# Attention backward for one query row: from one head per tile to two heads per tile

## The chip, the cores and the metric

The kernel runs on one core of a Trainium2 chip. The metric is the device time of one launch in microseconds (us); lower is better. The time before is the median of 3 runs, 1304.23 us (1302.53 to 1307.31). The profile is one further execution, taken by the hardware profiler.

## The reference

For each of 64 heads (B = 2, H = 32) there is one query row `q`, 8192 key rows `k` and value rows `v` of 128 numbers, and one row `grad_out`, all bf16. The forward part and its gradient are computed:

```python
def _fwd_reference(q, k, v):
    scale = q.shape[-1] ** -0.5
    scores = jnp.einsum("bhqd,bhkd->bhqk", q, k) * scale
    p = _softmax(scores, axis=-1)
    return jnp.einsum("bhqk,bhkd->bhqd", p, v)

def reference(q, k, v, grad_out):
    ...
    _out, _vjp = jax.vjp(_f, q, k, v)
    _grads = _vjp(grad_out)
    _out0 = jnp.asarray(_out)
    return (_out0, *[jnp.asarray(_g) for _g in _grads])
```

Written out for one head: p = softmax(scale * K q); out = p V; dp = V grad_out; dS = p * (dp - sum(p * dp)); grad q = scale * dS K; grad K = scale * dS x q (an outer product of 8192 by 128); grad V = p x grad_out (another). K and V, 2 MB each for a head, are read once, and grad K and grad V, 2 MB each, are written once: 537 MB in all.

## The kernel before

**Layout.** A head's 8192 rows lie on 128 partitions, 64 consecutive rows to a partition, so that a partition's share is 16 KB without a break, in memory and in the tile. `kt` and `vt` hold K and V of one head; the pool has five of each (`UNITS = 5`), 160 KB of a partition. The gradients are written over them: grad K over `kt`, grad V over `vt`, and each tile is stored from where it was loaded to. All four large transfers of a head move 2 MB in 128 rows of 16 KB.

**Queues.** SP issues the loads (line 103), `kt` then `vt`; ACT issues the stores (line 278). A load waits until the store of the head that had the buffer five heads earlier has landed.

**The order of the work** is written out by hand: one turn for each head `h` (64, and a last one to finish), of eight steps `j` with two halves `u`. In a turn, head `h` (called `y`) is transposed and its scores are formed, while the head before (`x`) gets its weighted sums, outer products and stores.

- `transposes` (lines 105 to 121): 8 matmuls by the identity write 8 blocks of 128x128 to the PSUM tile `tp` (two buffers), and one copy brings them to SBUF as `ev`: on ACT, or on DVE for two of the 16 halves of a head. Steps 0 to 3 are K, 4 to 7 are V.
- `products` (123 to 138), a step later: each transposed block is the stationary operand, and a column of q or grad_out the moving one; the results are columns of `sm` (scores) and `dp`.
- `row_max`, `all_max`, `exps` (157 to 181): after the K half, the maximum over the head, and exp of the scores into `E`, with its sum.
- `deltas`, `sums`, `weights` (190 to 231), in steps 0 and 1 of the next turn: the sum of E * dp, both sums over the partitions, and from them the weights of both weighted sums and the doubled columns `P2` and `dS2`.
- `weighted_rows` (233 to 247): 32 matmuls of 512 columns for a head, in steps 0 to 3 of the next turn, into `acc`, which gathers four heads before `acc_to_sbuf` and `combine` read it.
- `outer` (265 to 275): 8 multiplications on DVE for a head, 128x2048 each, in steps 1 to 6 of the next turn: four for grad V, then four for grad K. `store` is issued at j = 4 (grad V) and j = 7 (grad K).
- `spread_rows` (140 to 155): every four heads, the q and grad_out rows are copied to all partitions.
- At j = 7 the load of head h + 3 is written into SP's queue.

So both gradients of a head are made and stored in the turn after its own.

Of the kernel before, what the change touches and what calls it, by code (L numbers as in the profile page):

```python
# [9 lines left out]
ALU = mybir.AluOpType  # L10
# [6 lines left out]
QG = 4  # L17
OG = 4
UNITS = 5
# [3 lines left out]
def kernel(  # L23
# [10 lines left out]
):  # L34
    nc = tc.nc
# [5 lines left out]
    NT = Sk // P  # L41
    assert NT * P == Sk and NT == 4 * CH and BH <= P and BH % QG == 0
    assert BH % OG == 0 and OG * 8 == 32
    NS = 2 * NT // CH
    scale = float(D) ** -0.5

# [5 lines left out]
    ones_f = const.tile([P, P], F32)  # L52
    nc.vector.memset(ones_f[:], 1.0)

    pick = const.tile([P, 4, 2, OG], F32)
    idv = ident_f[:].rearrange("p (g w k j) -> p g j w k", g=4, w=2, k=OG)
    nc.vector.tensor_copy(out=pick[:], in_=idv[:, 0])
    for g in range(1, 4):
# [8 lines left out]
    evp = ctx.enter_context(tc.tile_pool(name="ev", bufs=5))  # L67
    work = ctx.enter_context(tc.tile_pool(name="work", bufs=2))
# [4 lines left out]

    k_v = k.rearrange("b h (p n) d -> (b h) p n d", n=NT)
    v_v = v.rearrange("b h (p n) d -> (b h) p n d", n=NT)
    dk_v = out_2.rearrange("b h (p n) d -> (b h) p n d", n=NT)
    dv_v = out_3.rearrange("b h (p n) d -> (b h) p n d", n=NT)

    acc = ps_one.tile([P, 4 * D], F32, name="acc", tag="acc")
    qT_all = const.tile([P, BH], BF16)  # L80
    doT_all = const.tile([P, BH], BF16)


    rl_all = const.tile([P, 2, BH], F32)

    wz = [
        [const.tile([P, NT // 4, 32], BF16, name=f"wz{w}{k}") for k in range(OG)]
        for w in range(2)
    ]
    colsT = const.tile([P, 2, BH], BF16)  # L90
    class Head:
        pass

    heads = [Head() for _ in range(BH)]

    def load(h):
        x = heads[h]
        x.kv = [
            kvp.tile([P, NT, D], BF16, name="kt", tag="kt"),
            kvp.tile([P, NT, D], BF16, name="vt", tag="vt"),  # L100
        ]
        for dst, src in zip(x.kv, (k_v, v_v)):
            nc.sync.dma_start(out=dst[:], in_=src[h])

    def transposes(h, j, u):

        x = heads[h]
        w, c = divmod(j, NS // 2)
        tp = ps_tp.tile([P, HC, P], F32, name="tp", tag="tp")
        for i in range(HC):  # L110
            n = c * CH + u * HC + i
            nc.tensor.matmul(  # L112
                tp[:, i, :], lhsT=x.kv[w][:, n, :], rhs=ident_bf[:], start=True, stop=True
            )
        ev = evp.tile([P, HC, P], BF16, name="ev", tag="ev")
        if u and j in (0, 7):
            nc.vector.tensor_copy(out=ev[:], in_=tp[:])  # L117
        else:
            nc.scalar.copy(out=ev[:], in_=tp[:])  # L119
        x.ev = getattr(x, "ev", {})  # L120
        x.ev[j, u] = ev

    def products(h, j, u):
        x = heads[h]
        w, c = divmod(j, NS // 2)
        if c == 0 and u == 0:
            if w:
                x.dp = ps_one.tile([P, NT + 2], F32, name="dp", tag="dp")
            else:
                x.sm = ps_one.tile([P, NT + P + 1], F32, name="sm", tag="sm")  # L130
        ev = x.ev.pop((j, u))
        col = (qT_all, doT_all)[w][:, h : h + 1]
        for i in range(HC):
            n = c * CH + u * HC + i
            nc.tensor.matmul(  # L135
                (x.dp if w else x.sm)[:, n : n + 1], lhsT=ev[:, i, :], rhs=col,
# [3 lines left out]
    def spread_rows(g):  # L140

        pb = ps_tp.tile([P, QG, 2, D], F32, name="pb", tag="tp")
        for i in range(QG):
            h = g * QG + i
            nc.tensor.matmul(
                pb[:, i].rearrange("p a d -> p (a d)"),
                lhsT=ident_bf[0:BH, h : h + 1].to_broadcast([BH, P]),
                rhs=nat[:].rearrange("p a d -> p (a d)"),
                start=True,
                stop=True,  # L150
            )
        qd = rowp.tile([P, QG, 2, D], BF16, name="qd", tag="qd")
        nc.scalar.copy(out=qd[:], in_=pb[:])  # L153
        for i in range(QG):
            heads[g * QG + i].qd = qd[:, i]

    def row_max(x):
        x.mp = work.tile([P, 1], F32, name="mp", tag="mp")
        nc.vector.reduce_max(out=x.mp[:], in_=x.sm[:, 0:NT], axis=AX.X)  # L159

    def all_max(x):
        mT = x.sm[0:1, NT : NT + P]
        nc.tensor.transpose(mT, x.mp[:], ident_f[:])  # L163
        x.gm = work.tile([1, 1], F32, name="gm", tag="gm")
        nc.vector.reduce_max(out=x.gm[:], in_=mT, axis=AX.X)

    def exps(x):
        mb = x.sm[:, NT + P : NT + P + 1]
        nc.tensor.matmul(mb, lhsT=ones_f[0:1, :], rhs=x.gm[:], start=True, stop=True)  # L169
# [4 lines left out]
        nc.scalar.activation(  # L174
            out=x.E[:],
            in_=x.sm[:, 0:NT],
            func=ACT.Exp,
            bias=negm[:],
            scale=scale,
            accum_out=x.ld[:, 0:1],  # L180
        )

    def to_weights(h, w, src):
        k = h % OG
        nc.vector.tensor_copy(  # L185
            out=wz[w][k][:, :, 16 * w + 4 * k : 16 * w + 4 * k + 4],
            in_=src[:].rearrange("p (m j) -> p m j", j=4),
        )

    def deltas(x):  # L190
        junk = work.tile([P, NT], BF16, name="junk", tag="junk")
        nc.vector.tensor_tensor_reduce(  # L192
            out=junk[:],
            in0=x.E[:],
            in1=x.dp[:, 0:NT],
            scale=1.0,
            scalar=0.0,
            op0=ALU.mult,
            op1=ALU.add,
            accum_out=x.ld[:, 1:2],  # L200
        )

    def sums(x):
        x.lsum = x.dp[:, NT : NT + 2]
        nc.tensor.matmul(x.lsum, lhsT=ones_f[:], rhs=x.ld[:], start=True, stop=True)  # L205

    def weights(h):
        x = heads[h]
        rl, rls = rl_all[:, 0, h : h + 1], rl_all[:, 1, h : h + 1]
        nc.vector.reciprocal(out=rl, in_=x.lsum[:, 0:1])  # L210
        negdelta = work.tile([P, 1], F32, name="negdelta", tag="negdelta")
        nc.vector.tensor_scalar(
            out=negdelta[:], in0=x.lsum[:, 1:2], scalar1=rl, scalar2=-1.0,
            op0=ALU.mult, op1=ALU.mult,
        )
        nc.vector.tensor_scalar(out=rls, in0=rl, scalar1=scale, scalar2=None, op0=ALU.mult)
        dSu = work.tile([P, NT], F32, name="dSu", tag="dSu")
        nc.vector.scalar_tensor_tensor(
            out=dSu[:], in0=x.dp[:, 0:NT], scalar=negdelta[:], in1=x.E[:],
            op0=ALU.add, op1=ALU.mult,  # L220
        )
        to_weights(h, 1, dSu)

        x.w2 = []
        for name, src, s in (("P2", x.E, rl), ("dS2", dSu, rls)):
            t = work.tile([P, NT, 2], BF16, name=name, tag=name)
            nc.vector.tensor_scalar(
                out=t[:], in0=src[:].unsqueeze(2).to_broadcast([P, NT, 2]),
                scalar1=s, scalar2=None, op0=ALU.mult,
            )  # L230
            x.w2.append(t)

    def weighted_rows(h, w, chunks):


        rows, k = heads[h].kv[1 - w], h % OG
        for c in chunks:
            for g in range(4):
                n = c * CH + 4 * g
                nc.tensor.matmul(  # L240
                    acc[32 * g : 32 * g + 32, :],
                    lhsT=wz[w][k][:, n // 4, :],
                    rhs=rows[:, n : n + 4, :].rearrange("p n d -> p (n d)"),
                    start=(w == 0 and k == 0 and c == 0),
                    stop=(w == 1 and k == OG - 1 and c == NT // CH - 1),
                    tile_position=(0, 32 * g),
                )

    def acc_to_sbuf(x):
        x.accsb = work.tile([P, 4 * D], F32, name="accsb", tag="accsb", bufs=1)  # L250
        nc.vector.tensor_copy(out=x.accsb[:], in_=acc[:])

    def combine(h):

        x = heads[h]
        c = ps_one.tile([P, 2, OG], F32, name="c", tag="c")
# [5 lines left out]
        own = slice(h - OG + 1, h + 1)  # L262
        nc.vector.tensor_mul(out=colsT[:, :, own], in0=c[:], in1=rl_all[:, :, own])

    def outer(h, w, i):

        x = heads[h]
        n = i * CH
# [6 lines left out]
        )  # L275

    def store(h, w, a=0, b=NT):
        nc.scalar.dma_start(out=(dv_v, dk_v)[w][h][:, a:b, :], in_=heads[h].kv[1 - w][:, a:b, :])

    def outer_and_store(h, w, i):  # L280

        outer(h, w, i)
        if h == BH - 1 and i % 2:
            store(h, w, (i - 1) * CH, (i + 1) * CH)
# [5 lines left out]
    for w in range(2):  # L290
        for t in wz[w]:
            nc.gpsimd.memset(t[:], 0.0)
# [4 lines left out]

    with tc.manual_schedule():
        for h in range(min(UNITS, BH)):
            load(h)  # L300
        for h in range(BH + 1):
            p = h - 1
            x = heads[p] if h else None
            y = heads[h] if h < BH else None
            full = h and p % OG == OG - 1
            for j in range(NS):
                for u in range(2):
                    if y:
                        transposes(h, j, u)
                    if u == 0:  # L310
                        if x and j == 1:
                            sums(x)
                        if y and j == 5:
# [67 lines left out]
```

## Time and profile before

| | |
|---|---|
| median of 3 runs | 1304.23 us |
| the profiled execution's own time | 1302.89 us |
| its span, first to last instruction | 1301.1 us |
| read from HBM, written to HBM | 268.47 MB, 268.47 MB |
| mean rate over the span | 415 GB/s |
| mean granted TensorE clock | 0.885 of full |
| copies `ev<-tp` on ACT | 896, 1025 ns each |
| copies `ev<-tp` on DVE | 128, 1224 ns each |
| outer products on DVE | 512, 1212 and 1216 ns each |
| weighted sums on PE | 2048, 415 and 476 ns each |
| issue to landing, median: `kt`, `vt`, store grad V, store grad K | 18.9, 28.5, 38.2, 40.3 us |

The page of a profile gives the busy time of each engine, the span cut in 40 slices with the DMA's share and rate, the DMA queues, the chain of work that ended last, the costliest groups of instructions with what each waited for, and the DMA issues with the time to landing. PE is TensorE's matrix multiplication, PEld its loading of the stationary operand, DVE VectorE, ACT ScalarE, SP the engine that only issues transfers. Large transfers are carried by 16 DMA engines, and each of them carries 8 of the 128 rows.

### The profile page before, as it was taken

How to read it: one execution, taken by the hardware profiler on the slowest of the kernel's cores; microseconds unless marked ns; L12 is line 12 of the kernel's file. 1: busy time of each engine (PE TensorE's matmuls, PEld its weight loads, DVE VectorE, ACT ScalarE, POOL GpSimd, SP SyncE). 2: the span in 40 equal slices, each digit the busy share in tenths (PEclk: the TensorE clock that was granted, in tenths of full speed). 3: DMA queues.
4: the chain of work that ended last, by engine and by line, in shares of the span. 5: the costliest groups of instructions: out<-in, count | busy, mean ns of one | idle time of the engine just before them, and what ended most of it. 6: DMA issues, size and time to landing. Idle time of an engine off the chain costs nothing.

```text
span 1301.1 us, 42243 instructions
## 1 busy us (share of the span) xinstructions
PE 1108.2 (85%) x18948; PEld 911.0 (70%) x18948; DVE 887.4 (68%) x1511; ACT 906.3 (70%) x1043; POOL 4.8 (0%) x16
## 2 busy tenths in 40 slices
PE   5999998988889879898898888988889888888784
PEld 5777777766767667677776767767767677677673
DVE  2887777766766767667676676766667667676566
ACT  5887778867767767676776766766668576676562
POOL 1000000000000000000000000000000000000000
PEclk9999989889887998888898888888899888898786
DMA  9999999999999999999999999999999999999986
GB/s 396 418 427 427 426 428 426 428 427 429 427 428 426 426 419 421 421 427 421 418 421 421 426 421 418 421 408 421 416 418 417 411 425 419 413 412 421 391 356 268
DMA packets 37653, 539.65 MB, mean 415 GB/s; under 512 B 4448, under 2 KB 4448, under 8 KB 4448
## 3 DMA queue, kind: packets, MB, share of 16 engines
q1 hardware_dynamic: 18432, 268.44, 49.6%
q10 hardware_dynamic: 19040, 268.51, 48.7%
q8 instruction: 148, 2.42, 0.7%
q14 instruction: 33, 0.27, 0.1%
HBM read 268.47 MB, written 268.47 MB: 413 GB/s over the span
## 4 chain that ended last, share of the span: by engine, by line
DMA 76%; PE 10%; ACT 6%; issue 4%; DVE 3%; ACTq 0%; DVEq 0%; SPq 0%
DMA out_dram<-kt 74%; PE tp L112 6%; ACT ev L119 5%; DVE ev L117 2%; PE acc L240 2%; DMA kt<-in_k_dram 1%; PE sm L135 1%; DMA nat<-in_grad_out_dram 1%; PE dp L205 0%; DVE kt L270 0%; DVE vt L270 0%; PE dp L135 0%; ACT E_f L174 0%; PE c L258 0%; PE sm L163 0%
## 5 line engine op out<-in xcount | busy, mean ns | idle before, releaser
L119 ACT CAST ev<-tp 128x1024 bf16<-128x1024 f32 x896 | 879.8, 1025 | 326.7 <-PE tp L112 270.7
L112 PE MATMUL tp<-ident_bf,kt 128*128 128x128 bf16 x4096 | 375.8, 245 | 83.3 <-DMA kt<-in_k_dram 54.8
L112 PEld LDWEIGHTS <-kt 128*128 128x128 bf16 x4096 | 281.1, 110 | 218.0 <-issue 156.4
L112 PE MATMUL tp<-ident_bf,vt 128*128 128x128 bf16 x4096 | 316.7, 221 | 60.4 <-ACT ev L119 44.3
L135 PEld LDWEIGHTS <-ev 128*128 128x128 bf16 x8192 | 332.4, 100 | 2.1 <-issue 0.2
L112 PEld LDWEIGHTS <-vt 128*128 128x128 bf16 x4096 | 260.9, 98 | 94.6 <-issue 74.2
L117 DVE CAST ev<-tp 128x1024 bf16<-128x1024 f32 x128 | 156.7, 1224 | 246.0 <-PE tp L112 237.3
L270 DVE TENSOR_TENSOR kt<-qd,dS 128x2048 bf16<-128x2048 bf16 x256 | 310.0, 1212 | 0.0
L270 DVE TENSOR_TENSOR vt<-qd,P 128x2048 bf16<-128x2048 bf16 x256 | 295.8, 1216 | 0.0
L135 PE MATMUL dp<-doT_all,ev 128*128 128x1 bf16 x4096 | 178.9, 165 | 0.1
L135 PE MATMUL sm<-qT_all,ev 128*128 128x1 bf16 x4096 | 178.6, 164 | 0.0
L240 PE MATMUL acc<-vt,wz 128*32 128x512 bf16 x1024 | 124.3, 476 | 9.3 <-DVE wz L185 9.2
L240 PE MATMUL acc<-kt,wz 128*32 128x512 bf16 x1024 | 108.2, 415 | 0.4 <-DVE wz L185 0.4
L240 PEld LDWEIGHTS <-wz 128*32 128x32 bf16 x2048 | 53.6, 95 | 21.7 <-DVE wz L185 12.4
L159 DVE TENSOR_REDUCE mp<-sm 128x1 f32<-128x64 f32 x64 | 14.4, 225 | 74.3 <-PE sm L135 74.3
L153 ACT CAST qd<-pb 128x1024 bf16<-128x1024 f32 x16 | 16.2, 1012 | 43.4 <-DMA out_dram<-kt 39.6
L210 DVE RECIPROCAL rl_all<-dp 128x1 f32<-128x1 f32 x64 | 10.8, 168 | 39.6 <-PE dp L205 39.6
L205 PE MATMUL dp<-ld,ones_f 128*128 128x2 f32 x128 | 28.4, 291 | 8.8 <-DVE ld L192 8.6
L205 PEld LDWEIGHTS dp<-ld,ones_f 128*128 128x128 f32 x128 | 24.8, 242 | 14.1 <-DVE ld L192 13.5
L171 DVE TENSOR_SCALAR negm<-sm 128x1 f32<-128x1 f32 x64 | 9.9, 154 | 23.9 <-PE sm L169 23.9
L169 PE MATMUL sm<-gm,ones_f 1*128 1x1 f32 x128 | 24.4, 257 | 0.0
L169 PEld LDWEIGHTS sm<-gm,ones_f 1*128 1x128 f32 x128 | 18.9, 184 | 6.7 <-issue 0.2
(40 smaller groups left out, 277.4 us busy)
## 6 DMA issues: line engine op xcount, KB each, us to landing
kt<-in_k_dram SPq DMA_DIRECT2D x64, 2048.0 KB, 18.9
vt<-in_v_dram SPq DMA_DIRECT2D x64, 2048.0 KB, 28.5
out_dram<-vt ACTq DMA_DIRECT2D x63, 2048.0 KB, 38.2
out_dram<-kt ACTq DMA_DIRECT2D x63, 2048.0 KB, 40.3
out_dram<-vt ACTq DMA_DIRECT2D x2, 1024.0 KB, 8.4
out_dram<-kt ACTq DMA_DIRECT2D x2, 1024.0 KB, 8.5
out_dram<-rows ACTq DMA_DIRECT2D x2, 16.0 KB, 7.4
nat<-in_q_dram ACTq DMA_DIRECT2D x1, 16.0 KB, 8.2
```

The source lines that it names most:

```text
L112: nc.tensor.matmul(tp[:, i, :], lhsT=x.kv[w][:, n, :], rhs=ident_bf[:], start=True, stop=True)
L117: nc.vector.tensor_copy(out=ev[:], in_=tp[:])
L119: nc.scalar.copy(out=ev[:], in_=tp[:])
L135: nc.tensor.matmul((x.dp if w else x.sm)[:, n : n + 1], lhsT=ev[:, i, :], rhs=col, start=True, stop=True,)
L153: nc.scalar.copy(out=qd[:], in_=pb[:])
L159: nc.vector.reduce_max(out=x.mp[:], in_=x.sm[:, 0:NT], axis=AX.X)
L169: nc.tensor.matmul(mb, lhsT=ones_f[0:1, :], rhs=x.gm[:], start=True, stop=True)
L171: nc.vector.tensor_scalar(out=negm[:], in0=mb, scalar1=-scale, scalar2=None, op0=ALU.mult)
L205: nc.tensor.matmul(x.lsum, lhsT=ones_f[:], rhs=x.ld[:], start=True, stop=True)
L210: nc.vector.reciprocal(out=rl, in_=x.lsum[:, 0:1])
L240: nc.tensor.matmul(acc[32 * g : 32 * g + 32, :], lhsT=wz[w][k][:, n // 4, :], rhs=rows[:, n : n + 4, :].rearrange("p n d -> p (n d)"), sta ...
L270: nc.vector.tensor_tensor(out=x.kv[1 - w][:, n : n + CH, :].rearrange("p n (d t) -> p n d t", t=2), in0=row.unsqueeze(1).to_broadcast([P, ...
```

## The change

Two heads, a pair, share a tile. Head 2i lies on partitions 0 to 63 and head 2i + 1 on 64 to 127, 128 consecutive rows of a head to a partition, so that a partition's share is 32 KB without a break. Every large transfer moves 4 MB in 128 rows of 32 KB. There are three tiles `kt` and three `vt` (`UNITS = 3`), 192 KB of a partition, and to make room `ev` has three buffers instead of five, and `work` one instead of two; `accsb` now takes a buffer of `ev`. The loads of the first pair are cut in four (K) and two (V).

A turn is one pair, with 16 steps: 0 to 7 transpose K, 8 to 15 V. `products` multiplies by the two columns of the pair at once; half of each result belongs to the other head and isn't read. What follows works on the rows of each head by itself (`own`, `halves`), so that many small instructions become two on 64 partitions, for a pair. Sums over the partitions use `same`, which is 1 where both partitions belong to one head.

The softmax sum is now formed by itself (`sum_exps`, step 11), so that P is known and `weighted_rows` for P runs in steps 12 to 15 of the pair's own turn. The outer products of grad V begin there too, and end in step 1 of the next turn. grad V is stored at step 3 of the next turn, grad K at step 8, and the load of pair i + 2 is written into SP's queue at step 9. `acc` is read after every pair. The stores of the last pair's pieces go out on SP's queue.

```diff
-UNITS = 5
+UNITS = 3
+EV = 3
...
-    k_v = k.rearrange("b h (p n) d -> (b h) p n d", n=NT)
...
+    def pairs_of(t):
+        rows = t.rearrange("b h s d -> (b h s) d")
+        return rows.rearrange("(i p n) d -> i p n d", p=P, n=NT)
+
+    k_v, v_v, dk_v, dv_v = (pairs_of(t) for t in (k, v, out_2, out_3))
...
+        for dst, src, parts in zip(x.kv, (k_v, v_v), (1, 1) if i else (4, 2)):
+            n = NT // parts
+            for a in range(0, NT, n):
+                nc.sync.dma_start(out=dst[:, a : a + n, :], in_=src[i][:, a : a + n, :])
...
-        if u and j in (0, 7):
+        if u and s in (8, 9, 10, 12):
             nc.vector.tensor_copy(out=ev[:], in_=tp[:])
...
-                (x.dp if w else x.sm)[:, n : n + 1], lhsT=ev[:, i, :], rhs=col,
+                (x.dp if w else x.sm)[:, 2 * n : 2 * n + 2], lhsT=ev[:, i, :], rhs=cols,
...
+    def own(t, k):
+
+        return t[halves[k], 0 : 2 * NT].rearrange("p (n k) -> p k n", k=2)[:, k]
...
+    def sum_exps(x):
+        x.lsum = x.sm[:, 2 * NT + P + 1 : 2 * NT + P + 2]
+        nc.tensor.matmul(x.lsum, lhsT=same[:], rhs=x.ld[:, 0:1], start=True, stop=True)
...
+    def to_weights(w, src, s):
+        for k, hf in enumerate(halves):
+            a = 8 * w + 4 * k
+            nc.vector.tensor_scalar(
+                out=wz[w][hf, :, a : a + 4], in0=src[hf, :].rearrange("p (m j) -> p m j", j=4),
+                scalar1=s[hf, :], scalar2=None, op0=ALU.mult,
+            )
...
+    def weights_v(x):
+        x.rl = work.tile([P, 1], F32, name="rl", tag="rl", bufs=2)
+        nc.vector.reciprocal(out=x.rl[:], in_=x.lsum)
+        to_weights(0, x.E, x.rl)
+        x.w2 = [twice("P2", x.E, x.rl[:])]
...
+    def weighted_rows(x, w, c):
+
+
+        for g in range(4):
+            m = 4 * c + g
+            nc.tensor.matmul(
+                acc[32 * g : 32 * g + 16, :],
+                lhsT=wz[w][:, m, :],
+                rhs=x.kv[1 - w][:, 4 * m : 4 * m + 4, :].rearrange("p n d -> p (n d)"),
...
     def acc_to_sbuf(x):
-        x.accsb = work.tile([P, 4 * D], F32, name="accsb", tag="accsb", bufs=1)
+        x.accsb = evp.tile([P, 4 * D], F32, name="accsb", tag="ev")
...
+    OUT_V = {13: (0,), 14: (1, 2), 15: (3, 4), 16: (5, 6), 17: (7,)}
+    OUT_K = {19: (0, 1), 20: (2, 3), 21: (4,), 22: (5, 6), 23: (7,)}
...
+        for i in range(NP + 1):
+            x = pairs[i - 1] if i else None
+            y = pairs[i] if i < NP else None
+            for s in range(NS):
                 for u in range(2):
                     if y:
-                        transposes(h, j, u)
+                        transposes(y, s, u)
                     if u == 0:
-                        if x and j == 1:
-                            sums(x)
...
+                        if x and s == 1:
+                            sum_deltas(x)
...
+                        if y and s == 11:
+                            sum_exps(y)
+                    if y and s:
+                        products(y, s - 1, u)
+                    elif x and s == 0:
+                        products(x, NS - 1, u)
+                    if x and 2 <= s < 6:
+                        weighted_rows(x, 1, 2 * (s - 2) + u)
+                    if y and s >= 12:
+                        weighted_rows(y, 0, 2 * (s - 12) + u)
+                if x and s == 0:
                     deltas(x)
+                if x and s == 1:
+                    weights_k(x)
+                if y and s == 8:
                     row_max(y)
+                if y and s == 11:
+                    weights_v(y)
+                    spread_rows(y)
+                for t, o in ((x, s + NS), (y, s)):
+                    if t:
+                        for w, at in enumerate((OUT_V, OUT_K)):
+                            for c in at.get(o, ()):
+                                outer(t, w, c)
+                if x and s == 6:
+                    acc_to_sbuf(x)
+                if x and s == 7:
+                    combine(x)
+                if x and x.i < NP - 1 and s in (3, 8):
+                    store(x, s // 8, nc.scalar)
+                if x and s == 9 and UNITS <= i + 2 < NP:
+                    load(i + 2)
```

## The prediction

> **What bounds the kernel now.** I read the page first, for the busy shares and the chain of work that ended last:
>
> ```profile
> PE 1108.2 (85%) x18948; PEld 911.0 (70%) x18948; DVE 887.4 (68%) x1511; ACT 906.3 (70%) x1043; POOL 4.8 (0%) x16
> ...
> q8 instruction: 148, 2.42, 0.7%
> ...
> DMA 76%; PE 10%; ACT 6%; issue 4%; DVE 3%; ACTq 0%; DVEq 0%; SPq 0%
> ```
>
> No engine is full, and three quarters of the chain are transfers. The chain in order of time has two regimes:
>
> ```profile
> 56.64 1.01 ACT ev L119
> ...
> 73.94 1.02 ACT ev L119
> ...
> 1011.59 40.25 DMA out_dram<-kt
> ...
> 1051.90 37.05 DMA out_dram<-kt
> 1088.96 3.42 issue
> 1092.37 40.41 DMA out_dram<-kt
> ```
>
> Up to 205 us it is computation, 17.30 us a head (56.64 to 73.94). From then on it steps from store to store, two heads each: 80.78 us for four heads (1011.59 to 1092.37), and 890.3 us for the 44 heads from 283.0 to 1173.3, so **20.23 us a head**. Computation has 2.9 us a head to spare there. What holds the DMA to 20.23 us? The windows:
>
> ```profile
> 100.00:200.00 100.00, 91.59 (x1667) 74.98 (x1666) 77.44 (x134) 78.84 (x90) 0.00 (x0) 0.97 1.01 427
> 1100.00:1200.00 100.00, 86.54 (x1507) 71.42 (x1504) 68.67 (x118) 71.45 (x83) 0.00 (x0) 0.90 1.00 416
> ...
> 1262.00:1264.00 2.00, 1.76 (x32) 1.26 (x28) 1.27 (x2) 0.42 (x2) 0.00 (x0) 1.00 1.11 475
> 1264.00:1266.00 2.00, 1.85 (x34) 1.41 (x34) 1.45 (x10) 1.16 (x2) 0.00 (x0) 1.00 0.56 229
> 1266.00:1268.00 2.00, 2.00 (x44) 1.63 (x40) 2.00 (x2) 1.90 (x3) 0.00 (x0) 1.00 0.08 33
> 1268.00:1270.00 2.00, 2.00 (x44) 1.56 (x40) 2.00 (x3) 1.90 (x3) 0.00 (x0) 1.00 0.06 25
> 1270.00:1272.00 2.00, 1.80 (x38) 1.51 (x37) 1.76 (x4) 1.95 (x3) 0.00 (x0) 1.00 0.10 33
> ```
>
> The last two columns are DMA share and GB/s. At 427 GB/s a head's 8.39 MB would take 19.6 us, and the rate falls later. From 1266 to 1272, 25 to 33 GB/s at a share of 0.06 to 0.10 is the work of one engine of 16 (427/16 = 27): fifteen have finished and wait for one. The packet records say the same all along: of a load's 16 end markers near 1005 us fifteen come by 1006.8 and the last at 1011.5, and these last ones follow at 1011.5, 1021.6, 1031.6 and 1041.6. So **one engine is late, and it sets the pace**. A 16 KB packet starts 607 ns after the one before on its engine, so 32 of them need 19.42 us a head; the late one needs some 0.8 us more. The likeliest extra is the instruction fetch (148 packets of 16 KB, 2.3 a head, each lasting 0.88 to 1.0 us); the change leaves the count of instructions as it is.
>
> The span of before is then: 2.3 us until data flow, 64 x 20.23 = 1294.7, and 4.1 at the end. The run took 1.8 us more than its span, and the median is 1.3 above that run.
>
> **The change, part by part.**
>
> *Rows of 32 KB.* The records give 306 ns from start to start for 8 KB packets and 607 for 16 KB, so one packet less saves 2 x 306 - 607 = 5 ns. A pair saves 32 of them on each engine, 0.16 us, and four end markers of 14 ns, 0.06 us: 40.46 - 0.22 = **40.24 us a pair**, 1287.7 for 32 (7 us gained). Bounds: no gain if the rows still go as 16 KB packets (7 us worse), and the 427 GB/s of the early windows if larger transfers free the kernel from its late engine (16.86 MB with fetches, 39.5 us a pair, 24 better).
>
> The Trainium skill, "SBUF — State Buffer", section "The DMA setup-cost knee", says that every transfer pays some 2 us whatever its size, so that larger ones gain. By that rule 128 transfers less would give 256 us; here transfers queue behind each other, at a share of 1.00, and the sum doesn't use it.
>
> *Compute in a pair's turn.* It must fit into 40.24 us. Rows of the compute-bound stretch: halves with `weighted_rows` start their transposes 1.06 us apart (35.45, 36.52, 37.58); the eight halves of V take 8.0 us; the wait for `sums` adds 0.8 a head. So two heads need 34.6. `products` stays 256 matmuls, bound by their weight loads (100 ns each, 165 with the matmul), so a second column costs nothing; `weighted_rows` stays 64 of 512 columns. Changed for a pair: one wait for sums less (-0.8). `combine` 8 matmuls, 1.04 us, for each pair and not for four heads (+0.5). In step 2 PE waits for `wz` of dS: DVE runs deltas (0.6), outers 5 and 6 (2.4) and weights_k up to `wz` (1.4) after the last products, 4.4 us; PE comes there after 3.3 (three halves and the sum): +1.1, with ACT's copies queued behind it. `accsb` holds an `ev` buffer through step 7, so copies wait for products (0.35 each) and step 8 for `combine`: +0.7, bounds 0 and 1.5. `spread_rows` now passes `tp` for each pair: +0.3. Two Exp with 0.24 us of accumulator reading are as many as before; strided reading of twice the columns adds 0.07 us to each of some ten: +0.7. Sum **37.1 us**, bounds 35.5 and 40: hidden by the DMA with 3.1 to spare, where before had 5.8. Without that cover each us costs 31. DVE's 16 outers and four copies stay (24.3 us a pair), the small operations go from 5.8 to about 5.6 us.
>
> The clock: after waits the granted clock is 0.50 (687 to 690 us, following a wait of 2.6 us), mean 0.86 to 0.90 in those stretches. A longer turn collects its slack in longer waits; until the slack is eaten that costs nothing. "TensorE: Matmul & The Clock Gate", Part 1, puts the fall to half rate after an idle window of about 3.4 us and says the same is needed to rise again. Every such window would cost 1.7 us, 41 us over 24 pairs if it were on the path; the slack takes it.
>
> *Filling.* Before, ten loads of 2 MB keep the DMA busy until stores come, and V follows K soon. Now a load of pair i + 2 waits for the store of grad K of pair i - 1. Compute starts at about 8.5 us, not 12 (the nat transfers pass 8 KB packets, not 16), turn 0 takes 35.7 (32 halves, no weighted sums in half of them), and grad V is issued 10.4 us into a turn, grad K 21.5. Loads of three pairs and both stores of pair 0, 33.6 MB, end at 81; the next store, V of pair 1, is issued at 44.2 + 37.1 + 10.4 = 91.7. So nothing is queued at 81, and from landing to data takes some 3.3 us (a load issued at 910.6 shows its first packets at 913.3). Likewise at 124.5 against 128.8, and at 168 against 165.9, nearly. **+7 us**, bounds 3 (a turn of 35.5) and 12. From pair 5 on a store is queued in time.
>
> *Moved loads and stores.* V and K stores on ACT's queue stand behind outer products that end by step 3 and 8 as DVE's times above add up; so no copies wait behind them. ACT's present waits there (39.6 + 16.7 us for landing stores) go, but were in turns that wait for `kt` anyway: 0.
>
> *End.* From the last load's issue (x) the late engine has 33.6 MB, 80.5 us. `kt` lands at x + 22; the last turn takes 38; then products 1.0, deltas 0.5, two outers 2.35, weights 1.8, nine outers 10.5 and accsb 0.7, and the last 1 MB store (now on SP's queue, where nothing else is left) needs 2.5 to its first packet, 2.5 for the data and 1.5 to land: x + 83.5. That is 3.0 beyond the late engine's own work, and the two small rows behind it add 1.5, as part of the 4.1 of before: **4.5 us**, bounds 0 and 12.
>
> **Sum:** 2.3 + 7 + 1287.7 + 4.5 = 1301.5 for the span, with 3.1 for launch and median 1304.6. Gains and costs cancel; as compute has less cover than before, I put the forecast at **1306**, with 1291 to 1319 as its own range (rows -0/+7, filling -4/+5, end -4.5/+7.5).
>
> **The rivals.**
>
> *Faster: the late engine no longer sets the pace.* For: 427 GB/s up to 400 us, and deeper queues. Against: its markers follow at 10.1 us early (201.6, 211.8, 222.0) and late. 32 x 39.5 + 2.3 + 7 + 4.5 + 3.1 = **1281**.
>
> *Slower: PE's turn sets the pace.* Place: steps 2 and 7 to 8, where PE waits in order for DVE and for `ev`. It decides from 39.8 us a turn on (44.2 + 31 x 39.8 + 24 + 3.1 = 1305), when my stalls are short by 2.7. At 41.5 us a turn: 44.2 + 31 x 41.5 + 24 (the end as above) + 3.1 = **1358**; at 40.5, 1327. For: three buffers of `ev`, and one order for all engines. Against: PE's 34.6 us for two heads, measured.
>
> *The rows are split into 16 KB packets*, so the change doesn't do what it says: 1304.6 + 5 = **1310**.
>
> **How the numbers follow.** Forecast 0.55, split rows 0.07, faster 0.18, slower 0.20. About 0.5% (6.5 us) is what a measurement of this kernel can tell from no change: 1297.7 to 1310.7. Of the forecast about 0.07 lies below that and 0.13 above; the split rows halve. Faster 0.25, same 0.39, slower 0.36. The range 1283 to 1338 leaves out some 0.1 on each side.
>
> **What would show it.** Right: data packets of 32 KB about 1.21 us apart; a chain of stores and loads at 40.2 us a pair after 230 us; one engine of 16 alone before the end; two or three gaps of 3 us near 81, 125 and 168; PE's waits for `wz` in step 2 near 1.1 us a pair. Wrong: a chain of PE and ACT late in the span (the slower rival), a period near 39.5 (the faster), or an idle DMA once for each pair, where a store of grad V comes after the landing of grad K.

## The result, and the profile after

After the change the kernel takes 1319.43 us (median of 4 runs, 1316.84 to 1322.95), before it 1304.88. The ratio is 1.0115, with a 95% interval of 1.0094 to 1.0135: **slower by 1.15%**, some 15 us. That lies inside the range that I gave (1283 to 1338), but 13 us above the forecast of 1306, and slower than the 1310.7 up to which, by the prediction, a measurement of this kernel can't tell a change from none. The profiled execution took 1320.59 us.

First its page: the span, the packets, the queues, and the issues with the time to landing.

```profile
span 1318.8 us, 42040 instructions
...
DMA packets 20371, 539.63 MB, mean 409 GB/s; under 512 B 2528, under 2 KB 2528, under 8 KB 2528
...
q8 instruction: 149, 2.44, 0.7%
...
kt<-in_k_dram SPq DMA_DIRECT2D x31, 4096.0 KB, 25.7
vt<-in_v_dram SPq DMA_DIRECT2D x31, 4096.0 KB, 43.5
```

The packets have almost halved (37,653 before): 15,872 of the records are of 32 KB, 1213 ns each in the median. The rows do go as they are written, so the rival of split rows is out. The instruction queue has one fetch more (149). The mean rate fell from 415 to 409 GB/s.

Next the issues of loads by SP: a load of `kt` is issued when grad K of the pair three before has landed, so the distance of two issues is the rhythm of the kernel (start in us, duration, queue, line, operation). The last line is an issue of ACT's queue, the store of grad V that went out nearest before the last load.

```profile
83.04 0.33 SPq L112 DMA_DIRECT2D kt<-in_k_dram  x1
...
126.49 0.33 SPq L112 DMA_DIRECT2D kt<-in_k_dram  x1
...
170.35 0.33 SPq L112 DMA_DIRECT2D kt<-in_k_dram  x1
```

```profile
1182.62 0.33 SPq L112 DMA_DIRECT2D kt<-in_k_dram  x1
...
1229.14 0.33 SPq L112 DMA_DIRECT2D kt<-in_k_dram  x1
...
1224.30 0.34 ACTq L291 DMA_DIRECT2D out_dram<-vt  x1
```

The reader is to see three stretches. The filling ends at 170.35. Then 26 pairs take 1229.14 - 170.35 = 1058.8 us, **40.72 us a pair**. From the last load to the end of the span there are 1318.8 - 1229.1 = **89.7 us**. My sum had 170.3, 40.24 and 85. (The span of 1301.5 with an end of x + 85 puts the last load at 1216.5, and 26 pairs of 40.24 before that is 170.3.) So the filling came out as forecast, and the miss has two terms: 26 x 0.48 = 12.5 us in the rhythm and 4.7 us at the end, 17.2 of the 17.3 us between the two spans. The rhythm is a mean of distances that swing: the last two are 37.5 and 46.5 us, and hold 3.6 of the 12.5.

The windows show the gaps of the filling, the long stretch, and the end (the last two columns are DMA share and GB/s).

```profile
78.00:86.00 8.00, 7.73 (x152) 6.43 (x150) 5.43 (x9) 7.28 (x8) 0.00 (x0) 0.99 0.69 260
122.00:130.00 8.00, 5.76 (x110) 4.66 (x106) 6.33 (x16) 5.99 (x7) 0.00 (x0) 0.96 0.64 241
400.00:1200.00 800.00, 690.51 (x11705) 574.46 (x11703) 562.57 (x811) 570.91 (x651) 0.00 (x0) 0.85 1.00 416
...
1264.00:1268.00 4.00, 4.00 (x51) 3.10 (x48) 3.69 (x4) 2.02 (x2) 0.00 (x0) 0.50 0.47 201
...
1288.00:1292.00 4.00, 4.00 (x80) 3.01 (x78) 2.48 (x3) 2.41 (x3) 0.00 (x0) 1.00 0.12 45
```

In the same three stretches before had 426, 428 and 419 GB/s. Near 81 and 124 us the DMA stands idle for a part of the time (shares 0.69 and 0.64), where before it didn't. At 1264 and 1290, in the last pair's turn, it is idle again for half of the time and more (0.47 and 0.12). The chain of work that ended last, which the prediction named as a sign, covers only 1% of the span on this page and settles nothing.

Last, PE's waits (total in us, times, longest) and, in order of time, where the last pair's turn begins.

```profile
PE acc L254 <- DVE wz L201: 54.2, 32, 3.7
PE tp L120 <- ACT ev L127: 45.7, 116, 0.8
PE tp L120 <- DMA kt<-in_k_dram: 31.4, 15, 4.5
```

```profile
1256.40 1.04 PE L120 MATMUL tp<-ident_bf,kt 128*128 128x128 bf16 x8 [4.49 <-DMA kt<-in_k_dram]
...
1297.29 0.28 DVE L224 CUSTOM_DVE_ANT_0 junk<-E_f,dp 64x128 bf16<-64x128 f32 x1 [0.86 <-PE dp L142]
```

PE waits for `wz` 54.2 / 32 = 1.7 us a pair, where I had 1.1, and 15 times for `kt` in 32 turns. The last turn could begin 27.3 us after its load was issued (1256.40 - 1229.14); I had 22.

### The profile page after: what moved, and what is told of

Its sections match the earlier page's. It is cut to its first block, busy times and chain, and to the rows that moved or that the text cites. A ratio compares the mean times of both kernels' runs of the same rounds, so it can differ in the third digit from the quotient of the medians.

```text
span 1318.8 us, 42040 instructions
## 1 busy us (share of the span) xinstructions
PE 1120.1 (85%) x19044; PEld 930.6 (71%) x19044; DVE 914.7 (69%) x1322; ACT 928.5 (70%) x1059; POOL 2.0 (0%) x10
## 5 line engine op out<-in xcount | busy, mean ns | idle before, releaser
L120 PE MATMUL tp<-ident_bf,vt 128*128 128x128 bf16 x4096 | 367.3, 242 | 39.5 <-ACT ev L127 29.2
L142 PE MATMUL dp<-doT_all,ev 128*128 128x2 bf16 x4096 | 181.4, 165 | 0.5 <-ACT ev L127 0.4
L142 PE MATMUL sm<-qT_all,ev 128*128 128x2 bf16 x4096 | 180.9, 165 | 0.9 <-issue 0.9
L254 PE MATMUL acc<-kt,wz 128*16 128x512 bf16 x1024 | 119.3, 461 | 54.2 <-DVE wz L201 54.2
L254 PE MATMUL acc<-vt,wz 128*16 128x512 bf16 x1024 | 109.5, 416 | 0.0
L254 PEld LDWEIGHTS <-wz 128*16 128x16 bf16 x2048 | 49.4, 86 | 67.6 <-DVE wz L201 55.0
L265 DVE COPY accsb<-acc 128x512 f32<-128x512 f32 x32 | 22.1, 692 | 31.2 <-PE sm L142 27.9
L271 PE MATMUL c<-pick,accsb 128*128 128x4 f32 x256 | 33.9, 256 | 6.6 <-DVE accsb L265 6.6
L271 PEld LDWEIGHTS c<-pick,accsb 128*128 128x128 f32 x256 | 31.8, 195 | 7.5 <-DVE accsb L265 7.5
L189 ACT ACTIVATE E_f<-sm,negm 64x128 f32<-64x128 f32 x64 | 23.2, 362 | 2.0 <-DVE negm L185 0.9
```

Of the source, the lines that this page charges most:

```text
L120: nc.tensor.matmul(tp[:, i, :], lhsT=x.kv[w][:, n, :], rhs=ident_bf[:], start=True, stop=True)
L142: nc.tensor.matmul((x.dp if w else x.sm)[:, 2 * n : 2 * n + 2], lhsT=ev[:, i, :], rhs=cols, start=True, stop=True,)
L189: nc.scalar.activation(out=x.E[hf, :], in_=own(x.sm, k), func=ACT.Exp, bias=negm[hf, :], scale=scale, accum_out=x.ld[hf, 0:1],)
L254: nc.tensor.matmul(acc[32 * g : 32 * g + 16, :], lhsT=wz[w][:, m, :], rhs=x.kv[1 - w][:, 4 * m : 4 * m + 4, :].rearrange("p n d -> p (n d) ...
L271: nc.tensor.matmul(c[:], lhsT=x.accsb[:, j * D : (j + 1) * D], rhs=pick[:, j], start=(j == 0), stop=(j == 3),)
```

## The experiments

Two theories stood against each other. **Mine:** one late DMA engine of 16 sets the pace, fetches of instructions make it late, and what the change lost over that are stretches in which too little is queued (filling, once a pair, end). **The rival:** the turn of PE, with its wait for `wz`, sets the pace.

### The transfers alone, without and with fetches

Four kernels, each run once, do only the transfers; all computation is left out, and copies of K and V are stored. Two of them add tiny matmuls, one column each, as many as bring the count of instructions near that of the whole kernel.

```
for i in range(N):                        # heads of 2 MB, or pairs of 4 MB
    for m in range(296):                  # dma16_pe; 592 a pair in dma32_pe
        nc.tensor.matmul(pt[0:32, m % 8 : m % 8 + 1], lhsT=ident_bf[:, 0:32],
                         rhs=kv[i][m % 2][:, 0, 0:1], start=True, stop=True)
    for w in range(2):
        nc.scalar.dma_start(out=(dv_v, dk_v)[w][i], in_=kv[i][1 - w][:])
    if i + UNITS < N:
        load(i + UNITS)
```

> The transfers of the kernel before alone: 2 MB in rows of 16 KB, five sets of tiles, every loaded tile stored where the gradient would go; no computation, so almost no instructions to fetch (the outputs hold copies of K and V). If the late engine is late because of instruction fetches: 64 heads x 19.48 us (32 packets of 607 ns and 4 markers) + 2.3 to start + some 3 to land = 1252 us, and no engine works alone at the end. If that engine is slow of itself or for another reason: 64 x 20.23 + 5 = 1300 us, with 25 to 33 GB/s in the last 5 us or more.

> The transfers of the changed kernel alone: 4 MB in rows of 32 KB, three sets of tiles, no computation (the outputs hold copies of K and V). If longer rows only save packets: 7 us less than the same with 16 KB rows, so 1245 us where that has 1252. If the longer rows or the three sets cost something of themselves (the 14 us that the change lost): 10 us or more above the run with 16 KB rows.

> The transfers alone with 16 KB rows, and beside them 296 tiny matmuls a head on TensorE (32 columns of weights, one moving column, results unused), which brings the number of instructions back to about that of the kernel before. If fetches make one engine late: 20.1 to 20.3 us a head, 1290 to 1300 us, and one engine alone at the end. If not: the same time as without the matmuls, within 5 us.

> The transfers of after (32 KB rows, 4 MB each) with 592 tiny matmuls for each pair, nothing else: all other computation is left out, and copies of K and V are stored. It has as many instructions as the earlier run of the 16 KB transfers with 296 matmuls a head, which took 1301.78 us against 1254.88 without them. Theory 1 (fetches make one DMA engine late, and a fetch costs that engine the same beside packets of 32 KB as beside 16 KB): the gain of the long rows, 7.6 us, stays: 1292 to 1296 us. Theory 2 (a fetch costs more beside longer packets, and this ate the gain that I forecast in after): 1299 to 1306, no better than with 16 KB rows.

| | time | span | pair's rhythm, from the issues of loads |
|---|---|---|---|
| dma16 (16 KB rows) | 1254.88 us | 1253.1 | 38.97 us |
| dma32 (32 KB rows) | 1247.29 us | 1245.5 | 38.75 us |
| dma16_pe (148 fetches) | 1301.78 us | 1300.0 | 40.41 us |
| dma32_pe (148 fetches) | 1297.12 us | 1295.3 | 40.38 us |

The rhythm of the second pair of kernels, from ends that lie 58 heads and 28 pairs of loads apart, with the load 16 pairs behind the first between them (dma16_pe, then dma32_pe):

```profile
61.08 0.33 SPq L56 DMA_DIRECT2D kt<-in_k_dram  x1
...
707.16 0.33 SPq L56 DMA_DIRECT2D kt<-in_k_dram  x1
...
1233.08 0.33 SPq L56 DMA_DIRECT2D kt<-in_k_dram  x1
```

```profile
67.62 0.33 SPq L56 DMA_DIRECT2D kt<-in_k_dram  x1
...
710.80 0.33 SPq L56 DMA_DIRECT2D kt<-in_k_dram  x1
...
1198.30 0.33 SPq L56 DMA_DIRECT2D kt<-in_k_dram  x1
```

(1233.08 - 61.08) / 29 = 40.41 us for two heads, (1198.30 - 67.62) / 28 = 40.38 for a pair. And the lone engine, in windows of dma16_pe, while the last loads are waited for:

```profile
1277.00:1279.00 2.00, 0.00 (x0) 0.00 (x0) 0.00 (x0) 1.00 0.08 33
...
1281.00:1283.00 2.00, 0.00 (x0) 0.00 (x0) 0.00 (x0) 1.00 0.06 25
```

What follows. **The instructions with their fetches cost 47 us** with 16 KB rows and 50 with 32 KB (1300.0 - 1253.1 and 1295.3 - 1245.5), and before, at 1301.1, stood 1.1 us above what its transfers take with them. That it is the fetch, and not the matmuls themselves, is argued: one engine of 16 is late, and the matmuls leave no other traffic. No run executes as many instructions without fetching them. A share of 0.06 is one engine of 16. **Over the whole run the long rows shorten the rhythm by 0.22 us a pair without fetches, just as I had it, and by 0.03 with them.** But that mean hides two stretches. In the first 16 pairs dma32_pe takes (710.80 - 67.62) / 16 = 40.20 us a pair and dma16_pe (707.16 - 61.08) / 16 = 40.38: the long rows keep 0.18. In the last 12 dma32_pe takes (1198.30 - 710.80) / 12 = 40.63, and the distances of its loads swing from 38.7 to 42.2 us, where before 710 they stayed between 39.9 and 40.4; dma16_pe takes 40.47. Why the loads begin to swing is not shown. By its total (1297.12) dma32_pe falls between the two theories of its expectation. By its first 16 pairs it is the first, since a fetch (some 4.6 a pair) costs about the same beside short and long packets: 40.38 against 38.95 in the same pairs without fetches, and 40.20 against 38.74, 0.31 and 0.32 us for each. The 4.7 us by which dma32_pe is ahead of dma16_pe are for the most part at the two ends of the run. A transfer fewer is worth little here: 128 of them with the longer rows gave 7.6 us, where an estimate from the 2 us that the Trainium skill, "SBUF — State Buffer", section "The DMA setup-cost knee", gives for each transfer would have 256.

One attempt to relieve the late engine failed.

```
-            nc.sync.dma_start(out=dst[:], in_=src[i])
+            for r in ((slice(0, 120), slice(120, 128)) if i % 13 == 6 else (slice(0, 128),)):
+                nc.sync.dma_start(out=dst[r], in_=src[i][r])
```

> The 16 KB transfers with 296 tiny matmuls a head (computation left out, copies stored; 1301.78 us), but of every 13th head both loads go as two pieces, partitions 0 to 119 and 120 to 127, so that the 8 rows of the second piece are dealt out over other engines than the last. If the late engine is the one that the last 8 partitions go to, it is relieved of some 3% of its packets: 1260 to 1285 us. If it is another engine, the others get more: 1300 to 1310.

It took 1341.72 us, 40 more than dma16_pe and worse than either theory had. After each of the five split heads the rate drops; near the last one:

```profile
1180.00:1200.00 20.00, 6.50 (x233) 6.37 (x233) 0.00 (x0) 1.00 0.84 243
1200.00:1220.00 20.00, 5.80 (x207) 5.56 (x203) 0.00 (x0) 1.00 1.01 420
```

The ten split loads left 70 end markers more, 23 for each and not 16, which fits pieces dealt out over 15 and 8 engines. The split disturbed the stream by itself, and which engine is the late one stays open.

### The queue and PE's turn

> The changed kernel with one difference: the load of the V tile is issued first, as soon as the store of grad V has landed (written into SP's queue at step 4), and the K tile's after the store of grad K (step 9, as now). Theory A, the queues run dry when grad K lands (two or three gaps while the pipeline fills, then a moment in each pair where grad V's store comes 2 to 4 us before or after that landing): the load of V fills these moments, and the time falls by 7 us in the filling and up to 12 later, to 1300 to 1308. Theory B, TensorE's turn with its clock falls sets 40.5 us a pair: the filling gains at most 7 and the rest nothing, 1312 to 1319. Theory C, the longer rows are slower of themselves: no change, 1317 to 1321.

```
-                if x and s == 9 and UNITS <= i + 2 < NP:
-                    load(i + 2)
+                if x and s in (4, 9) and UNITS <= i + 2 < NP:
+                    load(i + 2, (1,) if s == 4 else (0,))
```

(`load` now takes the tiles that it is to load.) The load of V goes out when grad V has landed, and no longer waits behind grad K: 1315.05 us (1312.78 to 1318.46), ratio to before 1.0086 (1.0067 to 1.0105). Its windows at the places where after had 260 and 241 GB/s:

```profile
78.00:86.00 8.00, 5.75 (x119) 4.90 (x116) 6.49 (x15) 6.79 (x8) 0.00 (x0) 1.00 1.02 436
122.00:130.00 8.00, 6.25 (x92) 4.62 (x93) 7.80 (x14) 4.69 (x5) 0.00 (x0) 0.79 1.04 444
400.00:1200.00 800.00, 682.45 (x11747) 568.28 (x11745) 563.10 (x814) 575.15 (x653) 0.00 (x0) 0.86 1.00 417
```

The gaps of the filling are gone: by 190 us the packets add up to 79.7 MB, as before (79.8), where after had 75.2. The rhythm is 40.51 us. Yet the median fell by 4.4 us only, and the two kernels' runs overlap. The time lies in the range of theory B, that TensorE's turn with its clock falls sets the pace: the up to 12 us that theory A had in the later rhythm didn't come.

> After, with outer products 5 and 6 of grad V moved behind the weights for grad K on VectorE, so that TensorE's wait for wz (1.7 us a pair in after) goes, while the store of grad V is issued some 0.5 us earlier or later in the turn. If TensorE's turn is what costs the 0.5 us a pair over my forecast (the rival): 8 to 25 us faster than after. If the late DMA engine or the nearly dry queue does: 0 to 3 us faster, or somewhat slower where the store of V comes later.

```
-    OUT_V = {13: (0,), 14: (1, 2), 15: (3, 4), 16: (5, 6), 17: (7,)}
+    OUT_V = {13: (0,), 14: (1, 2), 15: (3, 4), 17: (5, 6, 7)}
```

1316.98 us (1314.45 to 1318.89), which overlaps after's runs. The wait that was to go did go, from 54.2 us to 1.7, but two others came in its place:

```profile
PE c L271 <- DVE accsb L265: 44.3, 31, 9.0
...
PE tp L120 <- DMA vt<-in_v_dram: 24.1, 23, 2.4
...
PE acc L254 <- DVE wz L201: 1.7, 1, 1.7
```

In after PE waited for `accsb` 6.6 us and for `vt` 1.6. PE's busy time also grew, from 1120.1 to 1147.2 us, at a granted clock of 0.81 where after had 0.85. So PE's turn was not made shorter by 1.6 us a pair, and **the rival is not tested by this run.** Against it speaks that PE had to wait for the loads here in most turns. For it speak the turns of after in which PE waits for no load (times of four stretches, with DMA share and GB/s in the last two columns and PE's clock before them):

```profile
132.93:169.79 36.86, 31.97 (x600) 26.68 (x599) 28.14 (x42) 28.94 (x34) 0.00 (x0) 0.96 0.96 401
281.20:317.00 35.80, 30.94 (x600) 25.85 (x597) 28.06 (x41) 28.93 (x34) 0.00 (x0) 1.00 1.00 425
642.40:683.70 41.30, 36.66 (x595) 30.31 (x595) 28.65 (x41) 28.23 (x33) 0.00 (x0) 0.79 1.00 420
683.70:725.30 41.60, 36.66 (x599) 30.12 (x595) 28.65 (x41) 29.23 (x34) 0.00 (x0) 0.79 0.99 407
```

The first is from one store of grad V to the next, the others from the first transpose of a pair's K to that of the next. At a clock of 0.96 or 1.00 a turn takes 36 to 37 us, at 0.79 over 41. Of the 25 turns that begin between 239 and 1213 us, 14 end without a wait of more than 0.6 us for `kt`, and 12 of these take 40.2 to 41.9 us. In them PE's turn is as long as the transfers' 40.38, and no run shows which of the two sets the pace. (In the profile of wz_first the rhythm is 40.46 us, with grad V stored earlier in the turn.)

> After, with the store of grad V issued at the end of step 5 and not of step 3, some 4.5 us later in the pair's turn. In after it is issued 2 to 4 us before grad K of the pair ahead has landed. If the queues run nearly dry once a pair (my sign of error in the prediction), it now comes after the landing: the period rises by 2 to 5 us a pair in the steady stretch, 1360 to 1450 us in all. If the loads in the queue cover the gap, as with the late engine always busy: 1318 to 1326.

```
-                if x and x.i < NP - 1 and s in (3, 8):
+                if x and x.i < NP - 1 and s in (5, 8):
```

1340.12 us (1337.45 to 1350.44), ratio to before 1.0296 (1.0252 to 1.0341). Later by 4.5 us in its turn, the store of grad V costs 20.7 us in all; the rhythm is 41.53 us. The sign is that of the dry queue, but the period rose by 0.8 us a pair where I expected 2 to 5. SP and ACT's issues suggest why:

```profile
792.22 0.33 SPq L112 DMA_DIRECT2D kt<-in_k_dram  x1
...
835.78 0.33 SPq L112 DMA_DIRECT2D kt<-in_k_dram  x1
...
797.30 0.34 ACTq L291 DMA_DIRECT2D out_dram<-vt  x1
...
835.28 0.34 ACTq L291 DMA_DIRECT2D out_dram<-vt  x1
```

The store of V is issued 5.1 us after the landing (the issue of the load, 792.22) in one pair, and 0.5 before it in the next (835.28 against 835.78): only in some of the pairs can the queues run dry, and in those the late engine may still have work of its own while the others idle. So it is a matter of 0.8 us a pair in the mean, and after stands at the edge of it: its store of V is issued 4.8 us ahead of the last landing (1224.30 against 1229.14), 2 to 5 us in most pairs, and once 0.2 us behind it.

> vt_first (load of V issued when grad V has landed) and wz_first (outer products 5 and 6 of grad V behind the weights for grad K) together. vt_first alone took 1315.05 us, wz_first 1316.98, after 1319.4. If both only remove the stretches in which nothing is queued (the first by an earlier load, the second by an earlier store), their gains overlap: 1312 to 1316 us, with a steady period of 40.4 to 40.5 us a pair, that of the transfers alone with fetches. If they were independent, 4.4 + 2.4 us: 1312 to 1313, and if TensorE's turn set the pace, 1300 or less.

This is vt_first and wz_first together. 1318.56 us (1316.1 to 1319.68), ratio 1.0109 (1.0092 to 1.0127): no faster than either part. PE waits 41 us for `kt`, 22 times, and the rhythm is 40.65. The expectation was missed: what each seemed to gain in its own profile doesn't add up, so **the last 0.3 us of the rhythm of after isn't traced to one cause**.

### The size of the transfers

> After, with each transfer of 4 MB issued as two of 2 MB with rows of 16 KB, at the same points of the order. If long rows give in the whole kernel what they gave the transfers alone with fetches (1301.78 against 1297.12 us): 4 to 7 us slower than after, 1323 to 1327. If waits between the stages set the pace, or the half that lands early starts the next turn sooner: 0 to 4 us faster, 1315 to 1320.

```
-        for dst, src, parts in zip(x.kv, (k_v, v_v), (1, 1) if i else (4, 2)):
+        for dst, src, parts in zip(x.kv, (k_v, v_v), (2, 2) if i else (4, 2)):
...
-        queue.dma_start(out=(dv_v, dk_v)[w][x.i][:, a:b, :], in_=x.kv[1 - w][:, a:b, :])
+        n = (b - a) // (2 if b - a == NT else 1)
+        for e in range(a, b, n):
+            queue.dma_start(
+                out=(dv_v, dk_v)[w][x.i][:, e : e + n, :], in_=x.kv[1 - w][:, e : e + n, :]
+            )
```

1315.22 us (1314.6 to 1316.28), ratio 1.0085 (1.0066 to 1.0104). All four runs lie below all four of after. **With transfers of 2 MB in rows of 16 KB the changed kernel is 4 us faster, not slower** (the run changes the size of a transfer and the length of a row at once). Where? The rhythm is the same (40.67 us), and from the last load to the end it is 1314.5 - 1228.66 = 85.8 us in place of 89.7. The wait of PE's weight loads for `kt`, 36.7 us in after, is 4.1 here. A turn starts when half of K is there.

> both, and a shorter end: K of the last pair is loaded in four pieces of 1 MB, so that its turn need not wait for all 4 MB; the outer products of its grad V start in step 12 and not 13 and are all issued before the turn ends, one eviction goes to ScalarE for it, and acc is read out one step earlier. If the rest of the loss over the transfers alone (span 1295.3 us with fetches, against 1311 for vt_first) is the last pair's turn, during which too little is left to transfer: 6 to 11 us faster than both, 1302 to 1308. If it is lost in the steady stretch or to the late engine's own work: 0 to 3 us faster.

```
-            n = NT // ((1, 1) if i else (4, 2))[w]
+            n = NT // ((4, 2) if i == 0 else (4, 1) if i == NP - 1 else (1, 1))[w]
...
-        if u and s in (8, 9, 10, 12):
+        if u and (s in (8, 9, 10) or s == 12 and x.i < NP - 1):
...
+    LAST_V = {12: (0, 1), 13: (2, 3), 14: (4, 5), 15: (6, 7)}
...
-                if x and s == 6:
+                if x and s == (6 if y else 5):
```

Only the last pair differs from both (`combine` goes a step earlier too). 1310.82 us (1307.32 to 1313.37), ratio 1.0053 (1.0036 to 1.007): **7.7 us faster than both**. From the last load to the end: 1309.0 - 1225.25 = 83.8 us, and 89.0 in both, so 5.2 of the 8.9 us between the two spans were lost in the last pair's turn. The rest isn't the edit's: up to the last pair the two kernels are the same, and yet their rhythms are 40.42 and 40.65 us. Single profiles of one order of work lie that far apart, some 6 us in 26 pairs, and the rhythms above that differ by 0.2 us (40.46, 40.51, 40.65, 40.72) don't tell one edit from another. It is the fastest of the changed kernels, and still slower than before.

> What helped, put together: vt_first (1315.05 us), each load of K in two pieces of 2 MB (the last pair's in four of 1 MB), and the end of both_end; the outer products of grad V stay where after has them, since wz_first brought nothing beside vt_first (both took 1318.56). If the 4 MB grain of the loads is what costs the pairs their time (halves took 1315.2 against 1319.4 of after): TensorE's wait for kt, 41 us in 18 turns of vt_first, falls below 10 us, the span ends some 84 us after the last load of K is issued and not 86 to 90, and the time is 1303 to 1309, level with before. If the grain mattered at the end alone, or the gain of halves was that of its smaller stores: 1309 to 1313, as both_end.

```
-            n = NT // ((4, 2) if i == 0 else (4, 1) if i == NP - 1 else (1, 1))[w]
+            n = NT // ((4, 2) if i == 0 else (4, 1) if i == NP - 1 else (2, 1))[w]
```

Beside that, `OUT_V` is again that of after. I expected the best of all and got the worst but v_late: 1322.85 us (1320.34 to 1325.06), ratio 1.0134 (1.0113 to 1.0155). PE's wait for `kt` didn't fall, it rose:

```profile
PE tp L120 <- DMA kt<-in_k_dram: 62.3, 20, 7.5
```

The queues point to the reason, between 826 and 842 us, while the load of K (q1, rows of 16 KB) and the stores of both gradients (q10, rows of 32 KB) are under way (packets, MB, share):

```profile
q10 hardware_dynamic: 161, 4.75, 69.3%
q1 hardware_dynamic: 141, 2.10, 30.7%
```

Both queues get about as many packets, so the one with packets of half the size gets 2.10 of 6.85 MB. The Trainium skill, "DMA: Bandwidth & Descriptors", section "Queues, rings and completion order", says that an engine takes turns between its queues packet by packet (a packet there can hold several rows' worth of descriptors, a packet of the profile here is one row). These counts agree with equal turns, and show what follows: **shorter rows in one queue give the other queue the bandwidth.** A piece of K landed 34.7 us behind its issue in the median, where all of K took 25.9 in vt_first, and the stores of V slipped behind the landing of grad K in 25 of 26 pairs (in vt_first in none), as in v_late. In halves all queues had rows of 16 KB, and none lost.

## Why the prediction was off by 13 us

**One late engine sets the pace: right for the transfers alone.** dma16 and dma16_pe show the engine, and that it is late only beside the matmuls and their fetches (47 us). For after it is argued: its rhythm of 40.72 us lies 0.34 above that of the transfers alone. (The packet times in the prediction, such as 1006.8, 1011.5 and 913.3, lie 1.6 us late against the instructions' times. Their distances stay.)

**Rows of 32 KB, "40.24 us a pair": the first mis-sized term.** The 0.22 us that I took from the packets' starts are there when nothing else runs (38.97 to 38.75). With fetches dma32_pe kept 40.20 us for 16 pairs, as the sum had it, and then swung and took 40.63; its mean is 40.38. That is (40.38 - 40.24) x 26 = 3.6 us of the 12.5. So the step that failed is that one period, the same from the first pair to the last, was put for a stream whose loads swing, in after from 37.5 to 46.5 us. The other 0.34 us a pair, 8.8 us, are above what the transfers alone take, and are not traced. Both bounds that I gave for this term (no gain, or 39.5 us a pair) were on the better side of it: I had none for a loss.

**An idle DMA once for each pair**, which I named as a sign of error: v_late shows that a store of grad V behind the landing costs time. After stands at the edge of that, and its share in the 8.8 us isn't settled: vt_first and wz_first, each at 40.5, gave 40.65 together, and two profiles of one order of work differ by 0.23.

**Compute in a pair's turn, 37.1 us: right at a high clock.** In the stretch that computation bounds, two stores of grad V lie 169.79 - 132.93 = 36.9 us apart:

```profile
132.93 0.34 ACTq L291 DMA_DIRECT2D out_dram<-vt  x1
...
169.79 0.34 ACTq L291 DMA_DIRECT2D out_dram<-vt  x1
```

The wait for `wz` is 1.7 us and not 1.1. The term that I put at nothing is the clock: I had it cost nothing until the slack of 3 us is eaten. In the turns at 0.79 it is eaten, 41.3 and 41.6 us without a wait for a load. So the slower rival, PE's turn of 39.8 us or more, is neither shown nor out. PE's clock was lower in wz_first (0.81 over the whole, 0.85 in after) and the time no longer, but there PE waited for loads in most turns. The faster rival is out, as the rhythm came out longer.

**Filling, 7 us: right.** There are gaps near 81, 124 and 168 us, loads are issued at 83.0, 126.5 and 170.35, and the sum had 170.3 there. vt_first removes the gaps.

**End, 4.5 us: the second mis-sized term, 9.2 us.** The step that failed is "`kt` lands at x + 22". It took 27.3: the load shares the engines with grad V of the pair before, issued 4.8 us earlier, and with grad K, issued 4.9 us later, and its first packet was 4.0 us behind the issue (1233.2). That of the load behind the prediction's 3.3 us was 0.7 us behind its issue at 910.62, by the instructions' times. The turn that follows took 40.9 us up to deltas, where I had 39, and from there to the end it was 21.5, where I had 24: 5.3 + 1.9 - 2.5 = 4.7 us. halves (85.8 us from the last load to the end) and both_end (83.8) show that this is lost in the last pair's turn and can be had back.

The direction follows from these. Gains of 7 us were to stand against costs of 11.5. Instead the rhythm grew, from 40.46 us for two heads to 40.72, 6.8 us in 26 pairs. With 7 for filling and 5.1 at the end (9.2, where before had 4.1) that makes 18.9, and the six other pairs, which the sum takes at 40.24, give 1.3 back: 17.6 of the 17.7 us between the two spans. That the range held is in part luck, as its slower half was there for a rival and not for a rhythm that swings.

## What to carry to other kernels

Before a saving per packet is subtracted from a period, find what sets that period, and whether it is steady: here longer rows saved 0.18 us a pair beside fetches as long as the loads came at even distances, and nothing over the run. A larger tile is paid for at both ends of the run, because a turn starts when the whole transfer has landed; the size of a transfer and the size of the tile can be chosen apart. When transfers are cut, cut those of all queues alike, or the queue with the short rows loses its share. And a wait that an edit removes can come back in another place: read all waits of the engine, and its clock, before the run is taken as a test.

## What the runs showed of the hardware

Instructions are fetched by transfers of 16 KB, and 148 of them, 2.42 of 540 MB, come with 47 to 50 us of 1300 in kernels that only transfer. At the end of such a run one DMA engine of 16 works alone (share 0.06 to 0.08), and the last transfers wait for it. Matmuls of one column, 296 a head, whose results nothing waits for, took a kernel of copies from 1254.88 to 1301.78 us. Two queues share the engines by packets: 161 against 141, at 4.75 and 2.10 MB. And a turn of TensorE with the same work took 35.8 us at a granted clock of 1.00 and 41.3 at 0.79.
